# One k v product moved from the first feed-forward group into the last steps of a weight fold, and its loads moved ahead of three DMA transposes

## The chip, the cores and the metric

The kernel runs on one core of one Trainium2 chip. The metric is the device time in microseconds (us) of one execution. The core has a matrix engine (TensorE, PE in the profile, with its weight loads shown apart as PEld), a vector engine (VectorE, DVE), an activation engine (ScalarE, ACT), GpSimd (POOL) and a queue engine (SyncE, SP) that issues nearly all DMAs of this kernel. Each engine takes its own instructions in their order and waits on semaphores of the others.

## The reference

Linear attention over 8 batches, 8 heads, 576 tokens and head size 64, and behind it a feed-forward block with a product of two projections:

```python
kv = einsum('bhsd,bhse->bhde', k, v)             # 64 x 64 for each batch and head
o = einsum('bhsd,bhde->bhse', q, kv)
x = o / sqrt(mean(o * o, axis=-1) + 1e-6) * g    # norm over the head's 64 values
x = x.transpose(0, 2, 1, 3).reshape(4608, 512)
h = ((x @ w1) * (x @ w2)) @ w3                   # 512 -> 1024, 1024 -> 1024
return h @ w_out                                 # 1024 -> 512
```

The attention inputs are float32, the four weights float64. The result is 4608 x 512, float32.

## The kernel before

**Fold.** `w3 @ w_out` is formed first, from 8.7 us to 78.6 us, in two halves of eight steps `c`. A step turns one block of w3 (`turn_w3`, line 731, by PE, with the copy out of PSUM by ACT on line 733; or `w3_by_dma`, by a DMA transpose) and runs four groups of matmuls `fold_chunk` (line 747), which sum into four PSUM banks of the pool `ps_mm`. The weights come as float64 and are rebuilt as float32 by ACT (lines 171 and 176) and DVE (lines 181 to 193, with a scale on line 136).

**Attention of the first batch.** It is set between the steps of the second half. At `c = 4`: `begin_q` turns two q tiles by PE; `x_by_dma` takes the first half of the normed output apart on ACT (line 321) and turns it with two DMA transposes (line 325); `w3_by_dma(7)` does so for the last w3 block (DVE line 323, DMA line 325); then `begin_kv(1)` runs the second k v product on PE (line 362), copies it out of PSUM with six small ACT copies (lines 370 and 372), and issues the loads of k and v for the first half of batch 1 (line 105). At `c = 5`: DVE copies the two turned x parts to their place (`all_of(x_first)`, line 335), and `first.product(1)` runs the second q kv product on PE (line 440); its norm follows as a chain: two squares (ACT, 407), two reductions (DVE, 408), square root (ACT, 412), reciprocal and two multiplications (DVE, 414 and 417). ACT also copies the turned w3 block 7 between the squares and the root (line 335). At `c = 7`, behind the first of its four matmul groups, PE turns the normed output (`first.turn`, line 476).

**First feed-forward group.** `gates(0, p)` runs for p = 0 to 3 (line 778, seven products each), then `project`. For p of 1 to 3, and in `project`, a function `between` is called twice; each call takes the next of eight lists of attention steps of batch 1, `fs[0]` to `fs[7]` in `steps(1)`. `fs[0]`, taken within p = 1, holds `begin_kv(0)` of batch 1; `fs[2]`, taken within p = 2, holds its `begin_kv(1)` and its first q kv product.

**Order.** PE, POOL and SP follow the order in which the program is written throughout. In the fold, ACT and DVE do so too (`manual_schedule`); in the first group those two are ordered by the planner. The k and v tiles have one buffer each, so a load into them waits for the k v product that reads the old content. `begin_kv(g)` issues the next loads right behind its product:

```python
        def begin_kv(g, beside=None):
            kv(g, beside)
            if g == 0:
                load_four("kv", b, 1)
            elif b + 1 < B:
                load_four("kv", b + 1, 0)
```

The argument `beside` gives two PSUM banks to use; without it `kv` takes two from the pool `ps_at`, which has three. The pool `ps_mm` has five; four hold the fold's sums.

Of the kernel before, what the change touches and what calls it, by code (L numbers as in the profile page):

```python
# [22 lines left out]
def kernel(  # L23
# [54 lines left out]
    ps_mm = ctx.enter_context(tc.tile_pool(name="ps_mm", bufs=5, space=PSUM))  # L78
    ps_at = ctx.enter_context(tc.tile_pool(name="ps_at", bufs=3, space=PSUM))
# [5 lines left out]
    def bank(pool, tag):  # L85
        return pool.tile([P, 512], FP32, name=tag, tag=tag)
# [20 lines left out]
    def load_q_left(b):  # L107
        if b % 2 == 0:
            q_left[b // 2] = inp.tile([P, H, D], FP32, name="ql_sb", bufs=1)
        nc.sync.dma_start(  # L110
            out=q_left[b // 2][(b % 2) * L:(b % 2 + 1) * L],
            in_=q[b, :, G:S, :].rearrange("h p d -> p h d"),
        )
# [427 lines left out]
    def batch(b):  # L541
        if b not in batches:
            batches[b] = attention(b)
        return batches[b]
# [67 lines left out]
    def steps(b):  # L612

        a = batch(b)
        a.start()
        more = b + 1 < B
        fs, ends = ([[] for _ in range(8)] for _ in range(2))  # L620

        def turn(i, f, *args, next_group=False):

            t = []

            def begin():
                t.append(f(*args))
                next(t[0])
                if next_group and b == 1:
                    behind_store.append((next, t[0]))  # L630
                else:
                    next(t[0])

            fs[i].append((begin,))
            (to_end if next_group else ends[i + 1]).append((lambda: all_of(t[0]),))

        if to_end:

            ends[0] += [(lambda: nc.gpsimd.tensor_copy(tick, late["p5"][:, 0, 0:1]),), *to_end]
        to_end.clear()  # L640
        odd = b % 2
        by_scalar, in_two = b >= FIRST_OF_TWO, b > FIRST_OF_TWO
        if b == 1:
            early.extend(a.q_two_by_dma(r) for r in (0, 1))
            q_first = list(early)
            fs[0].append((a.begin_kv, 0))

            def end_first():
                for t in q_first:
                    with tc.issue_after(copies["u3"][-1].ins):  # L650
                        next(t)
                    all_of(t)

            ends[1].append((end_first,))
        def begin_first():
            rest = a.product(0)
            next(rest)
            slots.setdefault(("p1", "p1"), []).insert(0, (all_of, rest))

        left_of_last = not odd and b - 1 < LEFT_LATER  # L660
        left_now = odd and b >= LEFT_LATER

        def begin_left():
            left_norms.append(batch(b - 1).product_left(lambda o_ps: a.begin_kv(1, o_ps)))

        fs[2 if b == 1 else 1] += [
            (begin_left,) if left_of_last else (a.begin_kv, 1),
            (begin_first,) if by_scalar and not in_two else (a.finish, 0),
        ]
        if b == 1:  # L670
            last = {}

            def begin(name, behind, f, *args):
                last[name] = f(*args)
                with tc.issue_after(copies[behind][-1].ins):
                    next(last[name])
                next(last[name])

            def end(name, behind):
                with tc.issue_after(copies[behind][-1].ins):  # L680
                    next(last[name], None)
                all_of(last[name])

            fs[3] += [(begin, f"q{r}", "u3", a.q_two_by_dma, r) for r in (2, 3)]
            fs[3].append((begin, "left", "u3", a.q_left_by_dma))
            fs[4].append((begin, "x", "p1", a.x_by_dma, 0, nc.scalar.copy))
            ends[4] += [(end, "q2", "p1"), (end, "q3", "p5")]
            ends[5] += [(end, "x", "u2"), (end, "left", "u3")]
        elif by_scalar:
            turns_by_scalar(b)  # L690
        else:
            turn(1, a.q_two_by_dma, 2, 3)
            turn(2, a.x_by_dma, 0)
            if odd:
                turn(1, a.q_left_by_dma)
        second = 5 if b == 1 else 4
        if more and not left_now:
            fs[second].append((batch(b + 1).begin_kv, 0))
        fs[second].append((a.finish, 1))
        if left_now:  # L700
            kv_beside = (lambda o_ps: batch(b + 1).begin_kv(0, o_ps)) if more else None
            fs[3].append((lambda: all_of(a.product_left(kv_beside)),))
        if b == 1:
            turn(6, a.x_by_dma, 1)
        else:
            if not by_scalar:
                turn(5, a.x_by_dma, 1)
            if left_now or left_of_last:
                turn(5, batch(b if odd else b - 1).x_left_by_dma, next_group=more)
        if more and not by_scalar:  # L710
            turn(7 if b == 1 else 5, batch(b + 1).q_two_by_dma, 0, 1, next_group=True)
        if b == 1:
            fs[7].append((behind_store.append, (load_q_left, b + 1)))
        elif more:
            fs[7 if odd else 0].append((load_q_left, b + 1))
        return iter([lambda s=e + f: [f(*args) for f, *args in s] for e, f in zip(ends, fs)])
# [730 lines left out]
    with tc.manual_schedule(  # L1447
# [59 lines left out]
        BEGIN, PRODUCT = {1: 0, 4: 1}, {2: 0, 5: 1}  # L1507
        norms = {}
        FIRST = len(converted) + KF - 1
        turns, SPLIT = {}, {0: 3, 2: 5, 4: 7}  # L1510
        for c in range(KF):
            if c in BEGIN:
                first.begin_q(2 * BEGIN[c], 2 * BEGIN[c] + 1)
                if c == max(BEGIN):
                    x_first = first.x_by_dma(0, nc.vector.tensor_copy, split=nc.scalar.copy)
                    next(x_first)
                    next(x_first)
                    all_of(turns[c + 1])
            if c - 1 in norms:
                all_of(norms[c - 1])  # L1520
            if c < KF - 2:
                if c + 1 < max(BEGIN):
                    begin_next()
                elif c < max(BEGIN):
                    begun.append(conversions(len(begun)))
                    for steps_of_w in begun[-1]:
                        next(steps_of_w)
                if c == max(BEGIN) + 1:
                    for steps_of_w in begun[len(converted)]:
                        next(steps_of_w)  # L1530
                    all_of(x_first)
                else:
                    end_next(False)
                if c in SPLIT:
                    t = turns[SPLIT[c]] = w3_by_dma(SPLIT[c])
                    next(t)
                    next(t)
                if len(raws) < FIRST:
                    load_next()
                if c == 2:  # L1540
                    for steps_of_w in begun[len(converted)]:
                        next(steps_of_w)
                elif c == max(BEGIN):
                    run(sum_w(0))
            elif c == KF - 2:
                end_next(False)
            fold_chunk(1, c, [0])
            if c in BEGIN:
                first.begin_kv(BEGIN[c])
                if c == max(BEGIN):  # L1550
                    load_q_left(1)
            if c + 1 == KF:
                for r in range(2):
                    first.turn(2 + r)
                run(combine_x(0))
                end_next(False)
                for _ in range(3):
                    load_next()
            cut = NH - 2 if c == 1 else NH - 1
            fold_chunk(1, c, range(1, cut))  # L1560
            if c == 2:
                all_of(turns[c + 1])
            elif c + 1 < KF and c + 1 not in turns:
                turn_w3(1, c + 1)
                if c + 1 == max(BEGIN):
                    for steps_of_w in begun[-1]:
                        next(steps_of_w)
            if c in (max(BEGIN), KF - 2):
                begin_next()
            fold_chunk(1, c, range(cut, NH))  # L1570
            if c in PRODUCT:
                norms[c] = first.product(PRODUCT[c])
                next(norms[c])
                if c > max(BEGIN):
                    all_of(turns[c + 2])
                next(norms[c])
# [181 lines left out]
```

## Time and profile before

| | |
|---|---|
| median of 3 runs | 738.72 us (738.55 to 739.32) |
| the profiled execution's own time | 738.91 us |
| its span, first to last instruction | 736.8 us |
| PE busy | 731.3 us, 99% |
| DVE busy | 627.5 us, 85% |
| ACT busy | 381.1 us, 52% |
| mean granted TensorE clock | 1.000 |

Starts are in microseconds from the span's start. A line of the timeline gives the start, the length from the first start to the last end of like instructions in a row, the engine, the line of the program, the operation, the tiles out<-in, the shape and the count. A float32 matmul shows as two records, so a group of four matmuls over 512 columns shows as eight. Matmul records overlap; the pitch from one start to the next is what one costs. The idle time in brackets is that of the engine just before the instruction, with what ended it.

### The profile page before, as it was taken

Reading aid. Unit: us, or ns where it says so; the run is one execution under the profiler, and the core shown is the slowest. Engines: PE = TensorE matmul, PEld = TensorE weight load, DVE = VectorE, ACT = ScalarE, POOL = GpSimd, SP = SyncE. Lnnn points to the kernel's source line nnn. Section 1 sums busy time; section 2 is a strip of 40 time slices with the busy share of each in tenths; the row PEclk is TensorE's granted clock in tenths of the full one; section 3 lists DMA queues with packets and bytes.
Section 4 is the critical chain, followed back from the end, with each engine's and each line's share of the span. In section 5 each row is a group of like instructions: output and inputs, shape, how many; then the busy total and the mean of one; then the engine's idle time right before and its main releaser. Section 6 shows DMA issues by size and latency. Waiting matters only on the chain.

```text
span 736.8 us, 16930 instructions
## 1 busy us (share of the span) xinstructions
PE 731.3 (99%) x6873; PEld 658.4 (89%) x6873; DVE 627.5 (85%) x1259; ACT 381.1 (52%) x660; POOL 23.1 (3%) x30
## 2 busy tenths in 40 slices
PE   8999999999999999999999999999999999999998
PEld 6455788888899999999999999999999999999998
DVE  7988898868879689969996899689879987997797
ACT  7888778315652676167517761675177313212321
POOL 0000000220001000000010001000001000000000
PEclk9999999999999999999999999999999999999999
DMA  8999925599999598869987988698748862565454
GB/s 309 355 338 249 285 94 154 157 329 274 326 299 321 172 286 245 277 159 276 259 275 166 302 237 278 157 299 242 253 115 217 221 209 87 187 214 158 135 196 142
DMA packets 138769, 170.44 MB, mean 231 GB/s; under 512 B 81220, under 2 KB 114116, under 8 KB 138692
## 3 DMA queue, kind: packets, MB, share of 16 engines
q1 hardware_dynamic: 136240, 155.02, 71.4%
q10 hardware_dynamic: 2452, 14.35, 5.8%
q8 instruction: 54, 0.88, 0.5%
q14 instruction: 23, 0.19, 0.1%
HBM read 130.55 MB, written 20.71 MB: 205 GB/s over the span
## 4 chain that ended last, share of the span: by engine, by line
PE 98%; DMA 1%; DVE 0%; SPq 0%; issue 0%; ACT 0%; DVEq 0%
PE mm L778 37%; PE mm L1330 23%; PE mm L1072 21%; PE mm L747 8%; PE at L778 3%; PE at L362 3%; PE mm L440 1%; PE at L440 1%; PE at L731 1%; DMA raw<-in_moe_w_out_dram 1%; PE at L1373 0%; PE at L459 0%; PE at L382 0%; PE mm L302 0%; SPq L219 0%; PE at L476 0%
## 5 line engine op out<-in xcount | busy, mean ns | idle before, releaser
L1121 ACT COPY slots<-mm 128x512 f32<-128x512 f32 x88 | 51.6, 586 | 127.3 <-PE mm L1330 83.1
L778 PE MATMUL mm<-xT,w_sb 128*128 128x256 f32 x432 | 99.3, 379 | 0.0
L778 PEld LDWEIGHTS mm<-xT,w_sb 128*128 128x128 f32 x432 | 81.4, 190 | 11.1 <-issue 0.5
L778 PE MATMUL mm<-xc,ws 128*128 128x256 f32 x328 | 74.4, 379 | 0.0
L778 PEld LDWEIGHTS mm<-xc,ws 128*128 128x128 f32 x328 | 62.3, 190 | 8.5
L796 ACT COPY slots<-mm 128x512 f32<-128x512 f32 x58 | 34.0, 585 | 69.5 <-PE mm L778 64.7
L747 PE MATMUL mm<-chunks,ab 128*128 128x512 f32 (+1 forms) x136 | 59.2, 573 | 0.3 <-DVE chunks L193 0.3
L1125 DVE TENSOR_TENSOR slots<-mm,slots 128x512 f32<-128x512 f32 x66 | 45.2, 685 | 16.3 <-PE mm L1072 15.9
L1122 ACT COPY slots<-mm 128x384 f32<-128x384 f32 x88 | 42.3, 481 | 25.0 <-PE mm L1330 22.1
L1072 PE MATMUL mm<-ws,w3o_sb 128*128 128x128 f32 x350 | 54.0, 275 | 0.0
L1330 PE MATMUL mm<-w3o_sb,ab 128*128 128x128 f32 x368 | 48.8, 276 | 0.0
L408 DVE TENSOR_REDUCE inv<-sq 128x8 f32<-128x512 f32 (+1 forms) x40 | 24.6, 629 | 26.9 <-ACT sq L407 26.9
L1072 PEld LDWEIGHTS mm<-ws,w3o_sb 128*128 128x128 f32 x350 | 46.4, 192 | 0.0
L1330 PEld LDWEIGHTS mm<-w3o_sb,ab 128*128 128x128 f32 x368 | 45.4, 192 | 0.5
L1330 PE MATMUL mm<-w3o_sb,raw 128*128 128x128 f32 x340 | 43.5, 275 | 0.0
L747 PEld LDWEIGHTS mm<-chunks,ab 128*128 128x128 f32 x136 | 24.0, 190 | 21.0 <-issue 17.9
L1330 PEld LDWEIGHTS mm<-w3o_sb,raw 128*128 128x128 f32 x340 | 40.7, 192 | 0.0
L778 PE MATMUL mm<-xT,ws 128*128 128x256 f32 x160 | 38.1, 381 | 0.0
L1126 DVE TENSOR_TENSOR slots<-mm,slots 128x384 f32<-128x384 f32 x66 | 36.3, 551 | 2.0 <-PE mm L1330 1.9
L778 PE MATMUL mm<-xc,w_sb 128*128 128x256 f32 x152 | 36.6, 384 | 0.0
L778 PEld LDWEIGHTS mm<-xT,ws 128*128 128x128 f32 x160 | 30.1, 190 | 4.3 <-ACT slots L796 0.2
L335 ACT COPY xT<-xn 128x1024 uint16<-128x1024 uint16 x26 | 30.2, 1167 | 3.5 <-DMA xn<-xT 3.5
(247 smaller groups left out, 1664.3 us busy)
## 6 DMA issues: line engine op xcount, KB each, us to landing
w3o_sb<-w_l SPq DMA_DIRECT2D x21, 896.0 KB, 6.2
w3o_sb<-w3o_l SPq DMA_DIRECT2D x18, 896.0 KB, 6.6
raw<-in_moe_w_dram SPq DMA_DIRECT2D x31, 512.0 KB, 7.8
raw<-w3o_l SPq DMA_DIRECT2D x15, 896.0 KB, 4.9
w3o_sb<-w3o_l ACTq DMA_DIRECT2D x14, 896.0 KB, 4.8
k_sb<-in_k_dram SPq DMA_DIRECT2D x16, 576.0 KB, 4.9
v_sb<-in_v_dram SPq DMA_DIRECT2D x16, 576.0 KB, 5.8
q_sb<-in_q_dram SPq DMA_DIRECT2D x32, 256.0 KB, 5.4
```

Of the source, the lines that this page charges most:

```text
L335: copy(words(dst), src)
L362: nc.tensor.matmul(ps[r * D:(r + 1) * D, :], lhsT=k_sb[rows, r, cols], rhs=v_sb[rows, r, cols], start=(j == 0), stop=(j == JS - 1),)
L408: adds["norm"] = nc.vector.tensor_reduce(out=inv[:, i], in_=sq.rearrange("p (h d) -> p h d", d=D), axis=AX.X, op=ALU.add)
L747: nc.tensor.matmul(sums_ps[half][m][:, cols], lhsT=w3T[half, c][:, m, :], rhs=chunks[:, c, 1, cols], start=(c == 0 and cols.start == 0), s ...
L778: nc.tensor.matmul(ps[:, u, :], lhsT=lhsT(a_name, u, c), rhs=rhs(b_name, c),  start=(u == 0 and c == 0 and new), stop=(c == chunks - 1), s ...
L796: copies.setdefault(name, []).append(nc.scalar.copy(t, ps))
L1072: nc.tensor.matmul(ps[place // 4][:, place % 4, :], lhsT=x, rhs=y, start=new and place // 4 not in seen, stop=True, skip_group_check=True,)
L1121: nc.scalar.copy(z[:, 0:4], ps[0])
L1122: return nc.scalar.copy(z[:, 4:7], ps[1][:, 0:3])
L1125: nc.vector.tensor_add(z[:, 0:4], ps[0], z[:, 0:4])
L1126: nc.vector.tensor_add(z[:, 4:7], ps[1][:, 0:3], z[:, 4:7])
L1330: nc.tensor.matmul(ps[place // 4][:, place % 4, :], lhsT=x[:, c, :], rhs=y[:, c, :], start=new and place // 4 not in seen, stop=(c == 1), ...
```

## The change

`begin_kv(0)` of batch 1 no longer stands in `fs[0]` of `steps(1)`. It is called at `c = 5` of the fold's second half, right behind the matmuls of `first.product(1)` and ahead of the first step of its norm, with one bank of `ps_mm` and one of `ps_at`. At `c = 4` the issue of two DMA transposes of x and of one of w3 block 7 is moved behind `begin_kv(1)`, that is, behind the loads of k and v for batch 1, and stays ahead of `load_q_left(1)`.

```diff
@@ in steps(b), b == 1
             q_first = list(early)
-            fs[0].append((a.begin_kv, 0))
-
             def end_first():
@@ the fold's second half
                 if c == max(BEGIN):
                     x_first = first.x_by_dma(0, nc.vector.tensor_copy, split=nc.scalar.copy)
                     next(x_first)
-                    next(x_first)
                     all_of(turns[c + 1])
...
                     t = turns[SPLIT[c]] = w3_by_dma(SPLIT[c])
                     next(t)
-                    next(t)
+                    if c != max(BEGIN):
+                        next(t)
...
             if c in BEGIN:
                 first.begin_kv(BEGIN[c])
                 if c == max(BEGIN):
+                    next(x_first)
+                    next(turns[SPLIT[c]])
                     load_q_left(1)
...
             if c in PRODUCT:
                 norms[c] = first.product(PRODUCT[c])
+                if c > max(BEGIN):
+                    batch(1).begin_kv(0, [bank(ps_mm, "mm"), bank(ps_at, "at")])
                 next(norms[c])
                 if c > max(BEGIN):
                     all_of(turns[c + 2])
```

## The prediction

> **What bounds the kernel now.** I read the page first: the busy shares and the chain that ended last.
>
> ```profile
> PE 731.3 (99%) x6873; PEld 658.4 (89%) x6873; DVE 627.5 (85%) x1259; ACT 381.1 (52%) x660; POOL 23.1 (3%) x30
> PE 98%; DMA 1%; DVE 0%; SPq 0%; issue 0%; ACT 0%; DVEq 0%
> ```
>
> PE is nearly never without work (736.8 - 731.3 = 5.5 us), so a change pays by what it takes out of PE's row of matmuls and costs by the holes that it opens there. Next, PE's timeline at the three places that matter.
>
> ```profile
> 68.69 1.02 PE L747 MATMUL mm<-chunks,ab 128*128 128x512 f32 x2
> 69.64 1.16 PE L440 MATMUL at<-kv_sb,qT 64*64 64x64 f32 x64
> 70.74 4.56 PE L747 MATMUL mm<-chunks,ab 128*128 128x512 f32 x10
> 75.13 1.04 PE L476 MATMUL at<-ident,xn 128*128 128x128 f32 x8
> ...
> 92.40 3.62 PE L778 MATMUL mm<-xc,ws 128*128 128x256 f32 x16
> 95.94 1.28 PE L362 MATMUL at<-v_sb,k_sb 64*64 64x64 f32 x72
> 97.15 1.99 PE L778 MATMUL mm<-xT,ws 128*128 128x256 f32 x8
> 98.98 3.62 PE L778 MATMUL mm<-xT,w_sb 128*128 128x256 f32 x16
> ...
> 105.89 3.62 PE L778 MATMUL mm<-xc,ws 128*128 128x256 f32 x16
> 109.44 1.28 PE L362 MATMUL at<-v_sb,k_sb 64*64 64x64 f32 x72
> ...
> 111.58 1.99 PE L778 MATMUL mm<-xT,ws 128*128 128x256 f32 x8
> 113.41 3.62 PE L778 MATMUL mm<-xT,w_sb 128*128 128x256 f32 x16
> ```
>
> The first part is the product (L440) that the moved one is put behind, then ten fold records, then the turn (L476) of that product's normed output. The second is the moved k v product where it is now. The third is a k v and a q kv product in one burst, the arrangement that the change makes. Then the norm's chain on ACT and DVE, ACT's copies behind the burst of the third part, and SP's queue.
>
> ```profile
> 70.92 1.09 ACT L407 ACTIVATE sq<-at 128x512 f32<-128x512 f32 x2 [1.44 <-PE at L440]
> 71.89 1.16 ACT L335 COPY ab<-chunks 128x1024 uint16<-128x1024 uint16 x1
> 72.94 0.32 ACT L412 ACTIVATE inv<-inv,eps_col 128x16 f32<-128x16 f32 x1
> ...
> 112.17 0.20 ACT L370 COPY kv_sb<-at 128x64 f32<-128x64 f32 x1
> 113.49 0.60 ACT L407 ACTIVATE sq<-mm 128x512 f32<-128x512 f32 x1
> ...
> 70.04 1.30 DVE L335 COPY xT<-xn 128x1024 uint16<-128x1024 uint16 x2
> 73.64 1.29 DVE L417 TENSOR_TENSOR xn<-at,inv 128x512 f32<-128x512 f32 x2
> ...
> 64.02 2.59 SPq L325 DMA_TRANSPOSE xn<-xT  x2
> 66.72 1.92 SPq L325 DMA_TRANSPOSE chunks<-ab  x1
> 69.17 0.38 SPq L105 DMA_DIRECT2D k_sb<-in_k_dram  x1
> ```
>
> The norm's last multiplication ends at 73.64 + 1.29 = 74.93, and PE reaches the turn at 75.13: a slack of 0.20, of which some 0.07 goes to the semaphore (squares start 0.12 behind the product's last end, DVE steps 0.04 to 0.1 behind ACT's). This is the place to watch.
>
> **PE's own work.** Plain L778 records go at 0.2158 us (92.40 - 88.94 over 16 in the rows before). From 92.40 to 98.98 lie 24 of them, 5.18, in 6.58: the product alone costs 1.40 there, and that goes. From 105.89 to 113.41 are 7.52 less 5.18: both products in one burst cost 2.34. The q kv product alone in the fold: 68.69 to 75.13 is 6.44, less 12 fold records at 0.43 (5.16; their starts are 71.27, 71.70, 72.13 and so on), so 1.28. Behind it the moved product adds 2.34 - 1.28 = 1.06. PE's gain is 1.40 - 1.06 = 0.34; it reaches the turn at 75.13 + 1.06 = 76.19.
>
> **What the moved copies do to the norm.** ACT keeps the written order in the fold, so six copies of the k v product now stand ahead of the squares, and wait for the burst's end. That is 69.64 + 2.14 (109.44 to 111.58) = 71.78, plus 0.08 by which a burst's last records outlast the next start (95.94 + 1.28 against 97.15), and 0.12 to ACT: 71.98. From the first copy to the first square is 113.49 - 112.17 = 1.32, so squares start at 73.30 instead of 70.92: 2.38 later, where PE is 1.06 later. Behind the squares in ACT's queue stand the copy of turned w3 block 7 (to 75.4; fold step 7 wants it at 76.19 - 0.86 = 75.3, a wait that the later one for the norm covers), the root, two weight conversions and the copies of the turned x; DVE, next weights and x sums, waits on the root. All move together by about what PE moves.
>
> **The loads and the transposes.** SP is idle from 61.5 until ACT has x taken apart at 64.00. The moved k and v loads wait for the k v product that ends at 63.07, so they issue at about 63.15 and 63.6 and end at 64.05: the transposes issue as before, in 64.1 to 68.7. In the DMA engines they now queue behind 1.15 MB. By the trace's completion events the q loads ahead land at 66.63, the x transposes at 68.93 and 69.95, that of w3 at 70.85. Two k and v loads in a full queue took 1.28 and 1.50 (landings 57.16, 58.44, 59.94). So k and v land at about 67.9 and 69.5, before PE wants them at 70.7, and the transposes at 71.8, 72.8 and 73.7. DVE's two x copies, which both wait for the second one (the start at 70.04 is 0.09 behind 69.95), then run from 72.94; the reductions follow 1.21 + 0.03 on, at 74.18 instead of 71.55: 2.63 late, against 2.38 by ACT alone. The w3 landing at 73.7 is before ACT wants it (74.27).
>
> [...]
>
> With the root about 2.6 late (ACT's queue has room by 75.4), multiplications end at 74.93 + 2.58 = 77.51, seen by PE at 77.58; PE stands 77.58 - 76.19 = 1.39.
>
> **What else moves.** The loads of the second k and v half issue at about 72 instead of 97.31, ahead of six weight loads (from 70.84 before); SP waits there for the product's end, so these issue 2 us later. The first pair of them landed by 79.99 and is read at 81.05 (ACT), which itself moves by over 2 us; the queue had a gap from 70.85 to 72.6 that the new loads partly fill. I cost this at nothing; uncovered, it is at most the two loads, 2.8. POOL has no work here. The fifth `ps_mm` bank goes to the moved product, so the first group's first product takes the bank of the fold's first sum, copied at 75.39 + 0.58, about 78.5 afterwards, wanted at 81.0: free. In p = 1, where the product leaves, the next one accumulates in a bank whose copy (start 94.85, 0.56) ends at 95.41, wanted at 95.86: 0.4 of room, so the 1.40 comes back whole; ACT also loses 1.3 of copies.
>
> **Sum.** -1.40 + 1.06 + 1.39 = +1.05 us. On the profiled execution: 738.91 + 1.05 = 739.96. That execution lies 0.19 above the median of the runs shown (738.72), so 739.8 on the median.
>
> Ends: no stall at all is -0.34 (738.4). The upper end is a transpose behind k and v that lands late: the one issued at 52.79, which was queued behind a v load that landed at 59.94, landed at 62.39 (2.45 behind it, near the 2.30 I use), but after it the queue stood still again for about 1.2 us (hardly a packet started from 60.6 to 61.5). A second such pause within the three gives +1.2 us. I take the case without, as the three transposes before had one pause only.
>
> **The rivals.** Within 0.2%, 1.48 us, is about what a measurement of this kernel can tell from no change.
> - The forecast, norm late by about 2.6: between +0.5 (turn waits for half of the norm's output only, ACT alone binding) and +1.47. Chance 0.51. Its own range is 739.2 to 740.2.
> - The burst pays and the norm has room: -0.34, 738.4. For it: the k v burst costs less joined, by rows. Against: 0.20 of slack to a delay of 2.38 - 1.06. It needs the squares ahead of the copies. 0.10.
> - The transposes land late (the other side): DVE's copies and behind them the norm wait one for one. From x landing at 73.3 on (0.45 beyond my 72.8) the loss passes 1.48; with the pause of 1.2, 1.05 + 1.2 = +2.25, 741.0. For it the pauses at 58 to 61, against it the single pause of the same three. 0.22.
> - k or v is not there at 70.7: the k load issued at 49.97 took 8.5 to land; from 63.15 that is 71.65, 0.9 late, all moves by it: +1.95, 740.7. Against: the queue is shorter at 63. 0.08.
> - The 1.40 does not come back in p = 1 because ACT or DVE are now late there: +2.45, 741.2. Against: both were waiting for PE within p = 0 (1.51 DVE, 1.92 ACT). 0.06.
> - Faster by over 0.2%: all of PE's idle time is 5.5 us, 2.5 of it in the first 8.7 us, before any of this. 0.03.
>
> Faster 0.03; same 0.51 + 0.10 = 0.61; slower 0.36. The range 738.4 to 741.0 holds the first two and most of the third and fourth.
>
> **What would show it.** After: one burst of L440 and L362 at 69.64 with fold records 1.06 later; six L370 and L372 copies, then squares at about 73.3; DVE's L335 idle before it until about 72.9, released by DMA; PE idle before L476 of 1.2 to 1.5 us, released by DVE L417; no L362 between p = 1's products, L778 running on. Wrong if L476 starts with no idle time (second case), if DVE's x copies start after 73.4 (third), if L362 in the fold waits for DMA (fourth), or if PE stands within p = 1 (fifth).

## The result, and the profile after

The changed kernel takes 741.39 us (median of 5, 740.83 to 741.73) against 738.55 (738.34 to 739.32) for the kernel before, on the same chip: a ratio of 1.0035, 95% interval 1.0024 to 1.0046. It is slower by 2.84 us between the medians (2.6 by the ratio), where the forecast was no change that can be measured, and above the forecast's range (to 741.0). The profiled execution took 741.39, its span is 739.3 (before: 738.91 and 736.8).

PE's timeline of the changed kernel, at the places shown of before, and one more:

```profile
69.22 1.16 PE L440 MATMUL at<-kv_sb,qT 64*64 64x64 f32 x64
71.66 3.70 PE L745 MATMUL mm<-chunks,ab 128*128 128x512 f32 x8
76.64 1.13 PE L745 MATMUL mm<-chunks,ab 128*128 128x512 f32 x2 [1.28 <-ACT ab L335]
77.94 0.33 PE L476 MATMUL at<-ident,xn 128*128 128x128 f32 x1 [0.17 <-DVE xn L417]
78.53 0.98 PE L476 MATMUL at<-ident,xn 128*128 128x128 f32 x7 [0.27 <-DVE xn L417]
...
228.93 1.58 PE L1328 MATMUL mm<-raw,ab 128*128 128x128 f32 x12 [0.49 <-DMA raw<-w3o_l]
```

Before, none of these four waits is there. The burst takes 2.44 (69.22 to 71.66). Then PE waits first for ACT's copy of w3 block 7, which the forecast had only as covered by a later wait, and then for the norm. ACT, DVE and SP at the same place:

```profile
73.09 1.08 ACT L407 ACTIVATE sq<-at 128x512 f32<-128x512 f32 x2
75.44 1.16 ACT L335 COPY ab<-chunks 128x1024 uint16<-128x1024 uint16 x1 [1.26 <-DMA chunks<-ab]
76.50 0.30 ACT L412 ACTIVATE inv<-inv,eps_col 128x16 f32<-128x16 f32 x1
...
73.13 1.30 DVE L335 COPY xT<-xn 128x1024 uint16<-128x1024 uint16 x2 [3.53 <-DMA xn<-xT]
74.35 1.27 DVE L408 TENSOR_REDUCE inv<-sq 128x8 f32<-128x512 f32 x2
...
63.72 5.30 SPq L325 DMA_TRANSPOSE xn<-xT  x2
69.12 2.52 SPq L325 DMA_TRANSPOSE chunks<-ab  x1
```

The reductions end at 74.35 + 1.27 = 75.62. The root could start 0.04 behind them (that is the gap in the first experiment below), but ACT is then standing at its copy of w3, which waits for a DMA until 75.44; the root comes at 76.50, 0.84 late for that reason alone. The trace's completion events say why. The loads and transposes here report 16 times each, once for a share; in the trace's list of DMA packets a second kind stands beside the loads:

```
                       15 of 16 shares landed   last share
k, v (batch 1)              67.20  69.22         67.29  69.23
x, first and second         72.18  73.03         72.20  73.04
w3 block 7                  73.85                75.36
instruction packets of 16 KB: 67.86 to 69.87, 73.33 to 74.27
```

The line of the profile's page for those packets, in the changed kernel as in the one before:

```profile
q8 instruction: 54, 0.88, 0.5%
```

There are 54 such packets for 6873 pairs of weight load and matmul, one for every 127 pairs. They keep near to PE's count, not to the time: before, the two around the change ran at 67.08 and 86.21, when 465 and 597 of PE's matmuls had started; here they run at 67.86 and 73.33, when 468 and 613 had. So they are taken here for blocks of PE's program. The moved product of 72 pairs makes PE use up its program sooner in the fold, and the second block comes at 73.33, while w3's transpose is in flight: fifteen shares of it are there at 73.85, the last 1.51 later. That the one causes the other is tested below by moving the block.

PE's loss against before, point for point, is the table on which the experiments are read. It gives the start of the same matmul less its start before, both counted from the first batch's first q kv product (54.90 before), in us.

| kernel | first fold record behind the product | step 7 | turn, 2nd record | end of p = 1 | 246 | 730 |
|---|---|---|---|---|---|---|
| changed | 1.34 | 2.79 | 3.71 | 2.36 | 3.09 | 2.95 |
| changed, again | 1.80 | 2.92 | 3.85 | 2.50 | 2.50 | 2.36 |
| loads ahead only | 0.00 | 1.00 | 2.60 | 2.66 | 3.93 | 3.85 |
| burst only | 7.14 | 9.15 | 9.16 | 7.75 | 7.75 | 7.62 |
| 4 pairs less | 2.37 | 2.45 | 3.37 | 2.02 | 2.87 | 2.79 |
| 8 pairs more | 1.51 | 2.70 | 3.63 | 2.28 | 2.27 | 2.15 |
| copies behind squares | 1.56 | 2.62 | 3.55 | 2.20 | 2.20 | 2.37 |
| x copies last | 1.66 | 2.83 | 3.76 | 4.09 | 4.10 | 4.14 |
| w3 first | 1.80 | 1.88 | 5.30 | 5.40 | 6.35 | 6.56 |
| reordered | 1.34 | 1.34 | 1.34 | 0.86 | 1.06 | 1.34 |
| reordered, 6 pairs more | 1.69 | 1.69 | 1.69 | 0.29 | 1.34 | 1.60 |
| the same, again | 2.02 | 2.02 | 2.02 | 0.61 | 0.61 | 0.86 |

In the changed kernel the loss is 3.71 at the turn; 3.77 in p = 0 becomes 2.36 in p = 1, so 1.41 comes back. The first stretch of the kernel happened to run 0.42 faster than before's, and 0.73 is lost once more at 229: 2.36 - 0.42 + 0.73 - 0.15 = 2.52, the 2.5 by which the spans differ.

### The profile page after: what moved, and what is told of

Its sections match the earlier page's. It is cut to its first block, busy times and chain, and to the rows that moved or that the text cites. A ratio compares the mean times of both kernels' runs of the same rounds, so it can differ in the third digit from the quotient of the medians.

```text
span 739.3 us, 16928 instructions
## 1 busy us (share of the span) xinstructions
PE 731.7 (99%) x6873; PEld 658.7 (89%) x6873; DVE 628.0 (85%) x1259; ACT 381.7 (52%) x660; POOL 22.9 (3%) x30
## 4 chain that ended last, share of the span: by engine, by line
PE 95%; DMA 2%; ACT 1%; DVE 1%; SPq 1%; issue 0%; DVEq 0%; ACTq 0%
PE mm L776 37%; PE mm L1328 22%; PE mm L1070 21%; PE mm L745 6%; PE at L776 3%; PE at L362 2%; PE mm L440 1%; DMA chunks<-ab 1%; DMA raw<-w3o_l 1%; PE at L440 1%; PE at L729 1%; DMA raw<-in_moe_w_dram 1%; PE at L1371 0%; SPq L325 0%; PE at L459 0%
## 5 line engine op out<-in xcount | busy, mean ns | idle before, releaser
L794 ACT COPY slots<-mm 128x512 f32<-128x512 f32 x58 | 34.0, 586 | 69.5 <-PE mm L776 64.5
L745 PE MATMUL mm<-chunks,ab 128*128 128x512 f32 (+1 forms) x136 | 59.5, 574 | 1.3 <-ACT ab L335 1.3
L776 PEld LDWEIGHTS mm<-xc,w_sb 128*128 128x128 f32 x152 | 28.4, 190 | 4.0
```

Source lines behind the costliest of these rows:

```text
L745: nc.tensor.matmul(sums_ps[half][m][:, cols], lhsT=w3T[half, c][:, m, :], rhs=chunks[:, c, 1, cols], start=(c == 0 and cols.start == 0), s ...
L776: nc.tensor.matmul(ps[:, u, :], lhsT=lhsT(a_name, u, c), rhs=rhs(b_name, c),  start=(u == 0 and c == 0 and new), stop=(c == chunks - 1), s ...
L794: copies.setdefault(name, []).append(nc.scalar.copy(t, ps))
```

## The experiments

Three theories were set against each other. The copies theory: the six copies ahead of the squares make the norm late. (The forecast had these copies and x's landing, with x the later of the two, 2.63 against 2.38. So where the first expectation calls the copies alone the forecast, it gives only half of it: without them the forecast would still have had the norm late.) The queue theory: the loads ahead make the transposes late, and the waits that stand in ACT's and DVE's queue for them hold up the norm. The fetch theory: a 16 KB block of PE's program, on one of the 16 DMA engines, holds one share of a transpose.

**One half alone: the loads ahead, the product left in p = 1.**

```diff
             q_first = list(early)
+            fs[0].append((a.begin_kv, 0))
...
                 norms[c] = first.product(PRODUCT[c])
-                if c > max(BEGIN):
-                    batch(1).begin_kv(0, [bank(ps_mm, "mm"), bank(ps_at, "at")])
```

> The loads of k and v stay ahead of the three transposes, but the k v product goes back to p = 1, so no copies stand ahead of the squares and there is no burst in the fold. Copies theory (as forecast: the six ACT copies ahead of the squares are the price): no wait at the turn beyond 0.3 us, so 738.5 to 738.9. Queue theory (the loads make the transposes late, and the x copies on DVE and the w3 copy on ACT hold up the norm whether or not there is a burst): x lands at about 73.0 and w3 at 73.8 as in the changed kernel, the norm ends about 77.6, PE stands 2.5 to 3 us between fold step 7 and the turn, and nothing is saved: 741.2 to 741.7, no faster than the changed kernel. Fetch theory (one of the 16 DMA engines spends 1 us on a 16 KB block of PE's instructions while the w3 transpose is in flight, and PE asks for that block early because the burst uses up its instructions): as the queue theory, but w3 lands with all 16 shares together, since that block is asked for only at about 86 us.

Measured: 742.82 us against 738.98, ratio 1.0051 (1.0038 to 1.0063), as slow as the whole change or slower, and 1.1 above the range of the queue theory; in the profiled execution 1.27 is lost at 229 (2.66 to 3.93 in the table). PE, ACT and DVE of this kernel:

```profile
74.81 1.12 PE L746 MATMUL mm<-chunks,ab 128*128 128x512 f32 x2 [0.84 <-ACT ab L335]
76.78 0.33 PE L476 MATMUL at<-ident,xn 128*128 128x128 f32 x1 [0.84 <-DVE xn L417]
...
73.60 1.16 ACT L335 COPY ab<-chunks 128x1024 uint16<-128x1024 uint16 x1 [2.06 <-DMA chunks<-ab]
75.34 0.31 ACT L412 ACTIVATE inv<-inv,eps_col 128x16 f32<-128x16 f32 x1 [0.58 <-DVE inv L408]
...
72.82 1.30 DVE L335 COPY xT<-xn 128x1024 uint16<-128x1024 uint16 x2 [3.26 <-DMA xn<-xT]
74.03 1.27 DVE L408 TENSOR_REDUCE inv<-sq 128x8 f32<-128x512 f32 x2
```

No copy of the k v product stands ahead of the squares, which ran at 70.46, and yet the norm is 2.60 late at the turn. It is x, landed at 72.73, that holds DVE. Without the moved product the block comes at 87.76, w3's shares land together (73.52, lag 0.01), and the root waits for DVE, not for w3. So the order of the loads costs 2.6 by itself, with no copies of the moved product in the way, and w3's late share belongs to the moved product.

**The block's place: four pairs of PE's warm-up less.**

```diff
-        keep_warm(1, 12)
+        keep_warm(1, 10)
```

> The changed kernel with two of the small warm-up matmuls at 7 to 8 us left out, where PE waits anyway; nothing else differs, and no output depends on them. Two matmuls are four load and matmul pairs, so each later block of PE's instructions is asked for four pairs later. Fetch theory: the block asked for at 73.33 comes at about 75, behind the w3 transpose, so w3's last share lands with the other 15 at about 73.9 instead of 75.4; fold step 7 then waits 0.2 instead of 1.45, and as the norm is still held by the x copies to about 77.6 the whole gains 0.8: 740.5. Queue theory and copies theory: nothing changes, 741.4, and w3 lands at 75.4.

Measured: 741.62, ratio 1.0041 (1.0027 to 1.0054): no gain. The block of 73.33 went to 74.77, w3's shares landed together at 73.78 (lag 0.02), and the wait at step 7 is gone (2.37 to 2.45 in the table). But the block before it went from 67.86 to 69.96, and PE stood in the middle of the burst:

```profile
72.54 0.27 PE L362 MATMUL at<-v_sb,k_sb 64*64 64x64 f32 x1 [1.06 <-issue]
```

"issue" says that it waited for no semaphore. From 71.26 to 72.54 no matmul starts. In this kernel, in the changed one and in the reordered one below the gap is at the same place of PE's program, matmul 596 counted from the start, and ends 1.41, 1.41 and 1.33 behind the end of the 16 KB packet (71.13 to 72.54; 69.87 to 71.28; 70.53 to 71.86). PE runs 136 pairs in 2 us here; the reading that fits is that it reaches the end of the program it has been sent. So moving the block frees w3's share, as the fetch theory has it, and the block has a second price: late, it starves the burst.

Nor did the turn gain the 0.8 expected (3.71 to 3.37). The starved burst ended a microsecond later, and behind it the six copies and the squares, and now the reductions waited for these:

```profile
74.90 1.28 DVE L408 TENSOR_REDUCE inv<-sq 128x8 f32<-128x512 f32 x2 [0.53 <-ACT sq L407]
```

**The copies behind the squares.**

```diff
-                    batch(1).begin_kv(0, [bank(ps_mm, "mm"), bank(ps_at, "at")])
+                    copy_out = batch(1).begin_kv(0, [bank(ps_mm, "mm"), bank(ps_at, "at")], True)
                 next(norms[c])
+                if c > max(BEGIN):
+                    copy_out()
```

> The changed kernel with the six copies of the moved k v product written behind the two squares on ACT instead of ahead of them. Copies theory: squares 1.3 us earlier and the norm with them, 740.0 to 740.3. Queue and fetch theories: the reductions still wait for the x copies (x lands at 73.0) and the root for the copy of w3 (75.4), so squares move to about 71.8 and nothing else does: 741.2 to 741.6.

Measured: 741.25, ratio 1.0031 (1.0020 to 1.0043), the same as the changed kernel. The squares ran 2.37 earlier (each trace by its own clock), and nothing behind them moved:

```profile
70.72 1.09 ACT L412 ACTIVATE sq<-at 128x512 f32<-128x512 f32 x2 [1.44 <-PE at L445]
75.49 1.16 ACT L335 COPY ab<-chunks 128x1024 uint16<-128x1024 uint16 x1 [1.96 <-DMA chunks<-ab]
76.56 0.30 ACT L417 ACTIVATE inv<-inv,eps_col 128x16 f32<-128x16 f32 x1
```

DVE's x copies still started at 73.14. w3 had 15 shares at 73.87 and the last at 75.42, with a block at 73.40. The copies were hidden behind the two waits; as the price of this change the copies theory falls.

**Both ways around: w3 turned first, the copies behind the squares, DVE's x copies behind the norm's multiplications** (and for that the norm's output tile from the fold's pool).

```diff
+                    next(turns[SPLIT[c]])
                     next(x_first)
-                    next(turns[SPLIT[c]])
...
                 all_of(norms[c - 1])
+                if c - 1 > max(BEGIN):
+                    all_of(x_first)
...
-                    all_of(x_first)
```

> The changed kernel with everything out of the norm's way: the w3 transpose ahead of the two x transposes, the six copies behind the squares, and DVE's x copies behind the norm's multiplications (the norm's output gets a tile of its own, since the one buffer is still read by the x copies). Queue and fetch theories: w3 lands at about 71.5 to 72.5, x at 73 to 74 where nobody waits for it before 78; the norm is as early as before, no wait at fold step 7 or at the turn; PE's own saving of 0.34 less the 0.3 that the burst took longer than reckoned: 738.2 to 738.9. Copies theory: the same, since the copies are behind too. If it stays over 740, something else in the burst costs the time.

Measured: 739.68, ratio 1.0007 (0.9998 to 1.0016): level with before, though 0.8 above the expected range. Neither step 7 nor the turn waits (1.34 throughout): w3 landed at 72.71, before ACT's copy of it at 73.56, and x (74.36) is waited for only behind the norm. What is left is 0.28 of starving in the burst and a new wait, with which 0.93 is lost (1.34 less 1.41 would be -0.07 at the end of p = 1; it is 0.86):

```profile
86.09 1.99 PE L783 MATMUL mm<-xT,ws 128*128 128x256 f32 x8 [0.66 <-ACT slots L801]
...
84.40 1.16 ACT L169 ACTIVATE ab<-raw 128x1024 f32<-128x1024 uint32 x1 [1.75 <-DVE w_sb L188]
```

The same conversion starts at 82.95 in a later version of this kernel, where DVE's L188 begins after it (83.81), so it does not wait for DVE. It starts 0.10 behind the landing of its weights here and there (84.30 and 82.85). Here the block at 73.86 fell behind the last transpose, and the last share of the k and v loads and of four weight loads after them came 2.0 to 2.1 late.

**The other half alone: the burst in the fold, the loads left behind the transposes.**

```diff
-            fs[0].append((a.begin_kv, 0))
...
                 norms[c] = first.product(PRODUCT[c])
+                if c > max(BEGIN):
+                    batch(1).begin_kv(0, [bank(ps_mm, "mm"), bank(ps_at, "at")])
```

> One half of the change alone: both products in one burst in the fold, with the k and v loads left behind the three transposes. All theories: x and w3 land as before (69.95, 70.85), k and v not before 74.6 and 76.6, so PE stands in the burst from about 70.7 to 76.7, 6 us, and the squares, behind the k v product's copies, come as much later; 738.9 - 1.40 + 1.06 + 6 to 7 = 744.5 to 745.5.

Measured: 745.91, ratio 1.0088 (1.0063 to 1.0114), two executions, 0.4 above what was expected; v landed at 75.73.

```profile
75.87 0.33 PE L362 MATMUL mm<-v_sb,k_sb 64*64 64x64 f32 x1 [4.94 <-DMA v_sb<-in_v_dram]
```

That the time comes near the expectation is in part luck: the wait was 1.1 shorter than the 6 expected, and a cause comes in that no expectation has. After standing so long PE ran at half clock, from 75.28 to 82.10. A line of the table by stretches (start and end, length, busy time of PE, PEld, DVE, ACT and POOL, granted PE clock, DMA share, GB/s):

```profile
76.00:80.00 4.00, 4.00 (x75) 2.85 (x76) 0.00 (x0) 1.81 (x8) 0.00 (x0) 0.50 0.17 47
```

The halves can't be had one without the other: the loads have to be ahead for the burst, and ahead they are in the way of the transposes.

**Eight warm-up pairs more.**

```diff
-        keep_warm(1, 12)
+        keep_warm(1, 16)
```

> The changed kernel with eight more warm-up pairs of load and matmul at the very start, where PE waits anyway: nothing else moves but the point at which PE's next 16 KB block of instructions is asked for. Fetch theory: the block of 67.86 comes about 8 records earlier (64.5 to 66.5), early enough for the burst, which loses its gap of 0.20 at matmul 596 and takes 2.14; the block of 73.33 comes at the burst's end (71.0 to 72.0) and no longer holds the last share of the w3 transpose (whole by 73.9 instead of 75.36), so the wait of 1.28 at fold step 7 goes and the turn waits for x alone (landing 73.0, as after): 741.4 - 0.30 - 0.85 = about 740.2. If the block at 71 to 72 holds the two x transposes instead, x lands up to 1.3 later and the time stays at about 741.4. Queue theory (only the loads ahead of the transposes count): the landings and the time stay, 741.4.

Measured: 741.01, ratio 1.0027 (1.0017 to 1.0037): 740.2 was missed. The first block did come early, at 65.55, and the starving is gone. But it now lay on one share of the k load (15 shares at 67.39, the last at 68.93), v landed at 70.43 instead of 69.23, and the burst waited for it (a gap of 0.45). The second block came only 0.48 earlier, at 72.85, right behind the second x (72.78), and now all shares of w3 were late (75.20):

```profile
76.51 1.12 PE L745 MATMUL mm<-chunks,ab 128*128 128x512 f32 x2 [1.03 <-ACT ab L335]
```

So in these runs a block that moved put its price on another landing. From fifteen shares of k to fifteen of the first x are 4.98 us in the changed kernel and 4.47 when it ran again, 4.67, 4.46, 4.46 and 4.48 in the others with the order k, v, x (the block behind k's landing), and 4.52 here with the block in k. The sum is nearly the same wherever the block lay. No run had this stretch free of a block, so what share of it is the block's is not shown.

**The same eight pairs in the kernel before.**

```diff
-        keep_warm(1, 12)
+        keep_warm(1, 16)
```

> The kernel before with the same eight warm-up pairs more. It measures what a block of instructions costs a row of transposes. Before, the block of 67.08 lies in the first of three transposes, which took 2.30 against 1.02 and 0.90. Fetch theory: with the block asked for at about 63.5 to 65.5 the first takes about 1.0 too, x lands at about 68.6 instead of 69.95 and w3 at 69.5 instead of 70.85; the time stays (738.9), as nothing waits for them. Queue theory: the 2.30 is the change from ordinary loads to transposes and stays, wherever the block falls.

Measured: 738.80, ratio 0.9993 (0.9983 to 1.0003). This one tells nothing of the price: the block ran at 66.81, 0.45 behind the landing of the q loads (66.36), as it had before (66.63 and 67.08), and the first transpose took 2.29. Eight pairs did not move it; whether it was asked for earlier and held up in the DMA queue, the trace does not show.

**The reordered version with six warm-up pairs more.**

```diff
-        keep_warm(1, 12)
+        keep_warm(1, 15)
```

> The reordered version (w3 turned first, copies of the k v product behind the squares, the x copies behind the norm's multiplications) with six warm-up pairs more. There the block at 73.86 falls behind the last transpose and leaves one share of six weight loads 2.1 late; PE then waits 0.82 at 86. Fetch theory: the blocks come about 6 records earlier, the first in time for the burst (gap of 0.20 gone), the second by 72.5, ahead of the last transpose's landing, which evens the shares out again (lag of the weight loads under 0.5); the wait at 86 goes: 739.7 - 1.0 = about 738.7, level with before or 0.3 below it. If the wait at 86 has another cause (ACT's or DVE's later x copies), it stays and the time is 739.5.

Measured: 739.75, ratio 1.0008 (0.9999 to 1.0017), 1.0 above the 738.7 expected. The wait at 86 is gone, with the weight loads' last shares 0.1 late instead of 2.1, and the burst isn't starved, but v landed at 71.10:

```profile
71.24 0.24 PE L362 MATMUL mm<-v_sb,k_sb 64*64 64x64 f32 x1 [0.42 <-DMA v_sb<-in_v_dram]
...
227.62 1.58 PE L1335 MATMUL mm<-raw,ab 128*128 128x128 f32 x12 [0.81 <-DVE slots L1130]
```

The gap in the burst is 0.64, and by the end of p = 1 the loss is 0.29: without the wait for v it would be -0.35, where the burst was to bring -1.40 + 1.06 = -0.34. Then 1.05 is lost at 227. There the load that PE reads had 15 shares at 225.43 and the last at 227.49, 0.13 before PE went on, with a block at 221.41 ahead of it. (The line names DVE, but in the last profile below PE starts the same matmuls 0.95 before that instruction of DVE ends.) In the changed kernel the same load lagged by 1.55 and cost 0.73.

**x copies last, alone.** In the changed kernel, DVE's two x copies behind the multiplications, w3 still last.

```diff
                 all_of(norms[c - 1])
+                if c - 1 > max(BEGIN):
+                    all_of(x_first)
...
-                    all_of(x_first)
...
-            xn = st[h] = work.tile([P, 2, 2, 4, D], FP32, name="xn", bufs=1)
+            of = fold if (b, h) == (0, 1) else work
+            xn = st[h] = of.tile([P, 2, 2, 4, D], FP32, name="xn", bufs=1)
```

> The changed kernel with DVE's two copies of the turned x moved behind the norm's multiplications (the output tile of this norm comes from the fold's pool, so that nothing stands in a circle); w3 is still the last of the three transposes. Theory of two parallel causes (late x by way of DVE's queue, late w3 share by way of ACT's queue, both ahead of the root): the reductions start right behind the squares, at about 73.8 instead of 74.35, but the root still waits for ACT's copy of w3 at 75.44 + 1.16, so it stays at 76.5, the wait of 1.28 at fold step 7 stays, and the turn stays at about 78.4: no gain, 741.0 to 741.4. If x's late landing alone held up the norm, the root comes at about 75.0 and the turn at 77.0: 739.9.

Measured: 740.95, ratio 1.0022 (1.0011 to 1.0033). The reductions ran from 74.44 behind the squares alone. As the theory of two parallel causes had it, the root did not come sooner; ACT stood at w3 until 75.88, and then:

```profile
76.94 0.30 ACT L412 ACTIVATE inv<-inv,eps_col 128x16 f32<-128x16 f32 x1
```

In the table the loss at the turn is 3.76 against 3.71. (w3 landed whole at 75.80.) The profiled execution was one of 743.0, with its clock at 0.50 from 79.14 to 82.56, behind the turn; the other executions of this kernel were at 739.9 to 741.2.

**w3 first, alone.**

```diff
-                    next(x_first)
                     next(turns[SPLIT[c]])
+                    next(x_first)
```

> The changed kernel with w3's transpose issued ahead of the two of x; nothing else. Two parallel causes: w3 lands at about 72.2, the wait of 1.28 at fold step 7 goes, but the second x transpose is now last and lands at 73.9 or, with the block of PE's instructions on one of its shares, at 75.4; DVE's copies of x are still ahead of the reductions, so the root is at 76.5 (x at 73.9) to 78.0 (x at 75.4) and the turn at 78.4 to 79.9: no gain, 741.2 to 742.7. If the late w3 share alone held up the norm, the turn gains about 0.8: 740.5.

Measured: 744.10 (741.25 to 745.48), ratio 1.0067 (1.0043 to 1.0092), beyond the 742.7 expected. Step 7 no longer waits (1.88), but the block at 73.89 now held the last share of the second x, to 75.92, and DVE with it:

```profile
79.97 0.33 PE L476 MATMUL at<-ident,xn 128*128 128x128 f32 x1 [2.66 <-DVE xn L417]
```

And a line of the table by stretches, of the same kernel:

```profile
80.16:83.57 3.41, 3.14 (x10) 2.22 (x10) 3.27 (x5) 3.14 (x5) 0.00 (x0) 0.50 1.10 362
```

Behind that wait the granted clock was 0.50 for 3.41 us, and the loss went from 5.30 to 6.81. So either reordering alone gains nothing, and neither do the copies behind the squares alone. All three together gain 2.37 at the turn, 3.71 to 1.34. Late x and late w3 end at the same root, and the copies stand close behind them: with x out of the way (x copies last) and with w3 on time (four pairs less, with its burst a microsecond later) the reductions waited for the squares. No run has x and w3 cured and the copies still ahead.

**Two profiles again.** The changed kernel and the reordered one with six pairs more, each unchanged.

> The changed kernel again, for its profile: which of its waits come again in another execution. If the place of the blocks of instructions is set by the program, the fold comes out as before (block at 73.3 within 0.5, last share of w3 about 1.5 late, PE 2.36 behind by the end of the next stage, within 0.2). The extra 0.73 at 229, where the block at 223 fell on a share of the load that PE waited for, may come or not: 0 to 1.3, if which of the 16 engines carries a block is left to chance.

> The reordered version with six warm-up pairs more, again, for its profile: PE behind by 0.29 after the fold and the next stage (0.64 of it the wait for v in the burst, so -0.35 without it), and at 227 between 0 and 1.05 more. If the 1.05 at 227 comes again, it belongs to the program and not to the one execution.

Measured: 741.66 and 739.68. In the changed kernel the fold came out as before: block at 74.35 in an execution 0.85 later by its start, w3's last share 1.55 late, loss 3.85 at the turn and 2.50 by the end of p = 1. But the burst waited for v this time (landed at 71.62; the gap is 0.74) instead of starving. In the reordered version the wait for v was 0.96, and the loss by the end of p = 1 is 0.61, again -0.35 without it. The loss at 227 to 229 came in neither. It belongs to the single execution, and what decides it, such as the engine that carries the block, isn't settled.

No version beat the kernel before. The best that the reordering could reach, with neither starving nor waiting for v, is the 0.35 worked out above, less than these comparisons can tell from nothing.

## Why the prediction was wrong, point by point

- **PE's own work: right.** The pitch of 0.2158 fits longer rows; the 16 records named give 0.2163, which changes the terms by 0.01. The 1.40 came back as 1.41 (3.77 to 2.36). The burst's 1.06 is 1.05 where it is not starved (1.69 - 0.64 in the reordered version), 1.34 in the changed kernel; the 0.28 was not foreseen, but is covered there by the later waits.
- **The moved copies and the squares: right in size, without effect here.** Squares at 73.09, or 73.51 by before's clock, against 73.30. Putting the copies behind them changed nothing, as the forecast's own sum had it: there too x was the later.
- **k and v: right in the profiled execution, not in the next.** 67.29 and 69.23 (67.71 and 69.65 by before's clock) against 67.9 and 69.5 (the two pitches used give 69.41). When the same kernel ran again v landed at 71.62, 71.19 by before's clock, and PE waited for it in the burst. That is the sign of the fourth rival; its price was covered by the later waits (2.50 against 2.36 at the end of p = 1).
- **"The transposes issue as before, in 64.1 to 68.7": wrong.** They were issued from 63.72 to 71.64; with more in flight, the issue of one took up to 3.3. Nothing in the runs shows that this by itself cost time.
- **The landings: here the prediction failed.** The term is the 1.39 for standing at the turn, which rested on x at 72.8 and w3 at 73.7 "before ACT wants it (74.27)". PE stood 2.37 instead (1.34 to 3.71), and was 3.71 late at the turn, not 1.06 + 1.39 = 2.45. x landed at 73.46 by before's clock, 0.66 late, and w3 whole at 75.78, 2.1 late. By the rows of this kernel, 0.84 of the excess of 1.26 is w3's last share, which put the root off by that much, and the other 0.42 goes with x; no run has w3 on time and all else unchanged. Why x was late is not settled: from k to the first x the forecast had 3.9, and every run with this order took 4.5 to 5.0. For w3, what was left out is that the stretch now holds two blocks of PE's program where it held one. I had seen the pause in the first transpose (2.30 against 1.02 and 0.90) and taken it along once, without asking what it was. Before's trace has a block beside it (67.08 to 68.04) and one beside the pause that the prediction set aside (59.96 to 61.05), and none beside the 1.02 and 0.90; but it has a pause without a block as well, from 58.5 to 59.5. And I asked which engines and queues the moved instructions pass, but not what their number does to PE's own supply.
- **The later loads at nothing, the 1.40 back whole: right.** In the changed kernel PE does not wait in p = 0 or p = 1 after the turn.
- **The rivals.** The third came nearest: a second pause among the transposes, +2.25, 741.0, with 0.22. Its 2.25 is within about 0.1 of the fold's loss of 2.36, which is luck in part, as w3's share is no term of it. Its path, DVE's x copies from 73.4 on, is only half of it (73.13, or 73.55 by before's clock); the other half came through w3 and ACT's queue. "The norm has room" needed the squares ahead of the copies, and with just that it still did not come.
- **The transposes one by one.** After v, the first x took 2.97 here and the second 0.84, where the forecast took over 2.30 and 1.02 from before's landings. In both kernels the first of them, behind ordinary loads, took longest; why is not shown.

## What to carry to other kernels

Before work is moved into a stretch that lives on late transfers, list everything that waits in order ahead of the chain that sets the end, on every engine: here two waits, on two engines, with the copies close behind, so that curing one gained nothing. Count PE's records too: here one 16 KB block of program came for every 127 pairs, and a burst of 72 small pairs pulled the next block forward from 86.21 to 73.33, beside a transpose in flight whose last share then came 1.51 late. Where the room is 0.2 us, look at a DMA's last share, not at its mean rate.

## What the runs showed of the hardware that was not expected

- A 16 KB block of PE's program shows as one packet. The median of the 54 in the changed kernel is 0.96 us, the longest 2.02. Beside or behind several of them, a single share of a queued load or transpose was 1.3 to 2.2 late, and the loads behind it too (2.0 to 2.1 in the reordered version). ACT's copy of w3 waited for the sixteenth share: fifteen were there at 73.85, the last at 75.36, and the copy started at 75.44.
- In three traces PE stopped at the same matmul of the burst and went on 1.33 to 1.41 behind the end of a block's packet. The longest of these waits shows as "issue".
- The granted clock fell to 0.50 behind waits in three profiles, for 3.41 us with the x copies last and with w3 first, and for 6.83 with the burst alone. In the first two most of the 1.74 (3.76 to 5.50) and 1.51 (5.30 to 6.81) lost there is this. In the third it is about 2.9: 2.0 behind the product (7.14 to 9.15) and, of the 7.14, what 1.06 and the 5.15 from start to start at the wait (70.72 to 75.87) leave. In every trace the changes of the clock lie whole multiples of 3.41 us apart. From 9 us to PE's last work, cut by this grid, stretches at full clock with PE idle for 1.45, 2.66 and 3.41 us, in one piece or in several, were followed by a stretch at 0.50, and none with 1.28 or less was (the most was in loads ahead only and in 8 pairs more, PE busy for 2.13 of 3.41). The smallest that brought it, with the x copies last:

```profile
75.73:79.14 3.41, 1.96 (x5) 0.60 (x5) 1.76 (x4) 3.26 (x4) 0.00 (x0) 1.00 1.05 360
```

The changed kernel, run again, had waits of nearly the same sum (0.52, 0.97, 0.17 and 0.27, against 0.38, 1.01, 0.17 and 0.27), but the grid cut them apart: at most 1.06 fell into one stretch, and its clock stayed at 1.00. Idle time in a stretch can't be all of it: where PE's work ends, 1.55 (before), 1.76 (changed) and 1.90 (w3 first) in the last stretch with work brought no fall in the next. What decides it besides, these runs do not show.
